# Moving the early decode of seven weight halves to later units of the attention loop

## The chip, the cores and the metric

The kernel runs on one core of a Trainium2 chip. The metric is the device time of one execution in microseconds (us), as the median of three runs. The profiled execution is a single one with its own time. Engines are named as in the profile: PE (matmul), PEld (weight load), DVE (VectorE), ACT (ScalarE), POOL (GpSimd), SP (the engine that issues most DMAs).

## The reference, cut to what matters

Three layers follow each other: attention with rotary embedding (2 batches, 8 heads, 576 positions, 64 per head), a dense layer with softplus, and a mixture of 8 experts.

```
q_rot, k_rot = rotate(q), rotate(k)
scores = q_rot @ k_rot.T / sqrt(64); attn = softmax(scores); x = attn @ v     # [2, 8, 576, 64]
h = x @ w_in                      # x: [1152, 512], w_in: [512, 2048]
g = max(h, 0) + log1p(exp(-abs(h)))
x = g @ w_out                     # w_out: [2048, 512]
# then per token: skip gate, best of 8 experts, relu(x @ w1[e]) @ w2[e], scaled, added to x
```

The inputs w_in and w_out come as 64-bit floats. The kernel loads them as pairs of 32-bit words and makes 32-bit floats of them by shifts and masks; this is the decode of the change. Each decoded value is then split into a high and a low part of PE's rounded 32-bit type, so that products keep their precision.

## The kernel before

The attention works on 8 pairs of heads, (b, hp) = (0,0) to (1,3), and in each pair on 5 units of up to 128 query rows, so on 40 units, numbered 0 to 39. A pair is 5 units: unit 10 is the first of pair (0,2), unit 25 the first of (1,1), unit 35 the first of (1,3). For each unit PE makes the scores of two heads (s, L253), DVE takes the row maximum of each (m, L262), ACT the exponential (P, L275), PE transposes P (t, L344), ACT and DVE copy the transposed pieces out (pt, L88 and L90), and PE multiplies by v (pv, L388). DVE scales the result (x, L397). There are two buffers for scores.

The order on PE, DVE, ACT and SP inside a unit is written out by hand:

```
ORDER = "S0 R T0 M0 K H0 E0 S1 T1 M1 L E1 H1 W J T2 N H2 Q".split()
```

S is scores, M the maximum, E the exponential, T transposes, H copies, J the products with v, Q the preparation of the next pairs. Step W calls `side(i)`, which runs the jobs that the table W_AT gives to unit i. The preparation includes DMAs on SP that restack the keys and queries of the next pair inside SBUF: ks (4 DMAs of 288 KB, L219) and qs (4 of 128 KB); the scores of the next pair read both. POOL does the rotary embedding (rt, rot, remr) and some small steps.

W_AT has seven entries ((f, x), units). f is a block of 128 of the 2048 hidden columns, x = 0 is its part of w_in, x = 1 that of w_out. The units are those of the jobs load, decode (z = 0), decode (z = 1), high, low; the last three entries have only load and decode. The jobs are:

```
nc.vector.tensor_scalar(tu, hi, 3, 0x3FFFFFFF, ...)             # L549, decode z = 0
nc.vector.scalar_tensor_tensor(tu, hi, 0xC0000000, tu, ...)     # L550, decode z = 0
nc.vector.scalar_tensor_tensor(tu, lo, 29, tu, ...)             # L552, decode z = 1
self.nc.scalar.copy(self.w[f][:, x, 0, :], self.t[f, x])        # L557, high
self.nc.vector.tensor_sub(w[:, 1, :], self.t[f, x], ...)        # L561, low
```

A load (L536, L538) is one DMA of 512 KB on SP into a tile raw. There are two raw buffers and three of the decoded tile wt. The load's place on SP's queue is not the unit of the table: a scheduler puts a DMA where its buffer is free, and SP then issues in that order, waiting where it must.

After the last unit the dense layer begins. Its first matmuls (L583) use the halves decoded in the attention. High and low of the last three entries, and all of the other 25 halves, follow there.

Of the kernel before, what the change touches and what calls it, by code (L numbers as in the profile page):

```python
# [30 lines left out]
MORE = (2, 0, 8, 8, 0)  # L31

W_AT = (
    ((0, 0), (6, 10, 11, 11, 12)), ((0, 1), (8, 13, 14, 14, 15)), ((1, 0), (12, 16, 17, 17, 18)),
    ((1, 1), (15, 19, 20, 20, 21)), ((2, 0), (18, 22, 23)), ((3, 0), (21, 25, 26)), ((2, 1), (24, 28, 29)),
)

WARM = (15, 4, 4, 3, 6, 3)
# [1223 lines left out]
```

## Time and profile before

| | us |
|---|---|
| median of 3 runs | 523.63 |
| lowest to highest | 523.41 to 524.08 |
| profiled execution, its own time | 525.89 |
| its span, first to last instruction | 524.1 |
| PE busy in the span | 494.2 |
| DVE busy | 394.1 |
| ACT busy | 349.4 |
| POOL busy | 124.7 |

The busy times are sums over stages with different limits. The span is what the trace shows; the execution's own time has 1.8 us more around it. Times inside the trace are us from the span's start.

### The profile page before, as it was taken

What the parts mean: (1) busy time and instruction counts of PE and PEld (TensorE: products, weight loads), DVE (VectorE), ACT (ScalarE), POOL (GpSimd) and SP (SyncE); (2) the same over time, 40 slices, a digit from 0 to 9 for tenths busy, and PEclk for the clock granted to TensorE, in tenths of its full rate; (3) what the DMA queues carried; (4) which work ended last, traced back from release to release, by engine and by line L of the source; (5) the groups of instructions that cost most, each with busy time, mean ns of one, the idle gap of its engine ahead of it and who ended that gap; (6) DMA issues with size and microseconds to landing.
All of it is one profiled execution on the core that took longest, in us unless ns stands there. A gap on an engine that the chain in (4) does not pass through costs nothing. (4 is left out here: it accounts for less than half of the span.)

```text
span 524.1 us, 8652 instructions
## 1 busy us (share of the span) xinstructions
PE 494.2 (94%) x2926; PEld 397.4 (76%) x2927; DVE 394.1 (75%) x703; ACT 349.4 (67%) x802; POOL 124.7 (24%) x165
## 2 busy tenths in 40 slices
PE   7998989989899989999999999999989899999994
PEld 3676766667677668999999998998966577777773
DVE  7675898988765697899888965548855678787873
ACT  2575676766676668787777877666944487676860
POOL 0965796667122200000000000010002301220112
PEclk9999899999999999999999999999997999999998
DMA  7269576487420230233333323203253605995201
GB/s 168 74 175 223 131 218 170 109 229 170 125 70 2 85 93 33 81 121 121 120 117 110 106 72 110 91 2 106 81 174 82 273 1 202 324 336 150 80 21 38
DMA packets 41604, 65.47 MB, mean 125 GB/s; under 512 B 9184, under 2 KB 23776, under 8 KB 41552
## 3 DMA queue, kind: packets, MB, share of 16 engines
q1 hardware_dynamic: 37776, 57.89, 37.7%
q0 software_dynamic: 1440, 4.20, 2.2%
q10 hardware_dynamic: 2336, 2.74, 1.7%
q8 instruction: 26, 0.43, 0.3%
q14 instruction: 26, 0.21, 0.1%
HBM read 67.30 MB, written 7.15 MB: 142 GB/s over the span
## 5 line engine op out<-in xcount | busy, mean ns | idle before, releaser
L583 PE MATMUL h<-xh,w 128*128 128x320 f32 (+2 forms) x464 | 105.1, 309 | 0.0
L621 PE MATMUL acc<-w,gh 128*128 128x512 f32 x288 | 79.1, 397 | 4.5 <-ACT gh L611 4.5
L842 DVE TENSOR_TENSOR ws<-raw,ws 128x1024 fp32r<-128x1024 f32 x59 | 70.3, 1221 | 16.7 <-ACT ws L840 16.6
L583 PEld LDWEIGHTS h<-xh,w 128*128 128x128 f32 x464 | 78.0, 188 | 3.5 <-ACT r L598 0.3
L583 PE MATMUL h<-xl,w 128*128 128x320 f32 (+2 forms) x232 | 69.4, 308 | 0.0
L621 PEld LDWEIGHTS acc<-w,gh 128*128 128x128 f32 x288 | 51.7, 188 | 15.7 <-ACT gh L611 7.0
L262 DVE TENSOR_REDUCE m<-s 128x1 f32<-128x576 f32 x64 | 47.8, 752 | 19.7 <-PE s L253 16.1
L840 ACT CAST ws<-raw 128x1024 fp32r<-128x1024 f32 x59 | 59.2, 1060 | 2.4 <-DMA raw<-in_moe_w_dram 1.9
L930 PE MATMUL y<-ws,hT 128*128 128x512 f32 x216 | 59.8, 415 | 0.9 <-DVE ws L842 0.2
L275 ACT ACTIVATE P<-s,m 128x576 f32<-128x576 f32 x64 | 47.6, 749 | 15.9 <-DVE m L262 15.7
L596 ACT ACTIVATE y<-h 128x320 f32<-128x320 f32 (+2 forms) x58 | 25.4, 440 | 38.9 <-PE h L583 36.8
L253 PE MATMUL s<-ks,qs 128*128 128x288 f32 x224 | 44.3, 320 | 6.3 <-issue 2.5
L930 PEld LDWEIGHTS y<-ws,hT 128*128 128x128 f32 x216 | 39.2, 188 | 13.3 <-DVE ws L842 2.3
L344 PE MATMUL t<-ct,P 128*128 128x128 f32 x288 | 45.8, 278 | 3.2 <-ACT pt L88 2.1
L684 POOL TENSOR_SCALAR sc<-lg 128x2 f32<-128x2 f32 (+1 forms) x3 | 0.9, 291 | 196.8 <-DVE lg L667 196.8
L583 PEld LDWEIGHTS h<-xl,w 128*128 128x128 f32 x232 | 43.2, 188 | 2.1
L621 PE MATMUL acc<-w,gl 128*128 128x512 f32 x144 | 44.2, 392 | 0.1
L612 DVE TENSOR_TENSOR gl<-r,gh 128x256 fp32r<-128x256 f32 (+2 forms) x42 | 25.8, 614 | 22.7 <-ACT gh L611 21.8
L344 PEld LDWEIGHTS t<-ct,P 128*128 128x128 f32 x288 | 34.0, 141 | 10.3 <-issue 3.0
L253 PEld LDWEIGHTS s<-ks,qs 128*128 128x128 f32 x224 | 32.0, 191 | 11.8 <-ACT P L275 4.9
L88 ACT COPY pt<-t 128x384 f32<-128x384 f32 x60 | 28.1, 481 | 17.5 <-PE t L344 17.4
L388 PE MATMUL pv<-pt,vr 128*64 128x256 f32 (+1 forms) x256 | 37.1, 412 | 0.0
(264 smaller groups left out, 956.0 us busy)
## 6 DMA issues: line engine op xcount, KB each, us to landing
raw<-in_moe_w_dram SPq DMA_DIRECT2D x68, 512.0 KB
raw<-in_moe_w_in_dram SPq DMA_DIRECT2D x16, 512.0 KB
raw<-in_moe_w_out_dram SPq DMA_DIRECT2D x16, 512.0 KB
ks<-kT SPq DMA_DIRECT2D x28, 288.0 KB
qs<-qT SPq DMA_DIRECT2D x28, 128.0 KB
wr<-in_moe_w_dram SPq DMA_DIRECT2D x5, 512.0 KB
x2d<-x SPq DMA_DIRECT2D x9, 256.0 KB
xn<-in_q_dram SPq DMA_DIRECT2D x8, 256.0 KB
```

Source lines behind the costliest of these rows:

```text
L88: self.nc.scalar.copy(out, in_)
L253: nc.tensor.matmul(ps[:, c, 0:288], lhsT=qs[:, a, uc], rhs=ks[:, a, x, 288 * c : 288 * c + 288], start=x == 0, stop=x == 1,)
L262: self.last = nc.vector.tensor_reduce(st["m"][:, a : a + 1], st["ps"][a][:, :, 0:288], axis=AX.XY, op=ALU.max, negate=True)
L275: nc.scalar.activation(P[:, 576 * a : 576 * a + 576].rearrange("p (c n) -> p c n", c=2), ps[:, :, 0:288], AF.Exp, bias=m[:, a : a + 1], ac ...
L344: self.tail = nc.tensor.transpose(ps[:, 128 * i : 128 * i + 128], src, ident)
L388: nc.tensor.matmul(ps[r, 0:n], lhsT=v, rhs=pt[:, k, 0:n], start=i < 0, stop=i == 3, skip_group_check=True,)
L583: nc.tensor.matmul(ps[c][:, 0:m], lhsT=w[:, 0, x, 128 * k : 128 * k + 128], rhs=src[:, k, c0 + m * c : c0 + m * c + m], start=z == 0, stop ...
L612: self.last = nc.vector.tensor_sub(gl, r, gh.bitcast(F32))
L621: nc.tensor.matmul(acc[t], lhsT=g[x][:, 128 * j : 128 * j + 128], rhs=w[:, 1, y, :], start=f == f0 and z == 0, stop=f == f1 and z == 2,)
L840: hi = nc.scalar.copy(w[:, 0], raw)
L842: self.did[T, c] = hi.ins, nc.vector.tensor_sub(w[:, 1], raw, w[:, 0].bitcast(F32)).ins
L930: nc.tensor.matmul(py, lhsT=ht[:, x, o : o + 128], rhs=w[:, y, 512 * j : 512 * j + 512], start=c == 0 and j == 0 and z == 0, stop=c == 3 a ...
```

## The change

The seven entries keep their jobs and their order; the units move later. A half that was loaded at unit 6 and decoded at 10 and 11 has its load at 18 and its decode at 24 and 25, and so on; the last decode moves from unit 29 to 37.

```
 W_AT = (
-    ((0, 0), (6, 10, 11, 11, 12)), ((0, 1), (8, 13, 14, 14, 15)), ((1, 0), (12, 16, 17, 17, 18)),
-    ((1, 1), (15, 19, 20, 20, 21)), ((2, 0), (18, 22, 23)), ((3, 0), (21, 25, 26)), ((2, 1), (24, 28, 29)),
+    ((0, 0), (18, 24, 25, 25, 26)), ((0, 1), (20, 26, 27, 27, 28)), ((1, 0), (25, 28, 29, 29, 30)),
+    ((1, 1), (27, 30, 31, 31, 32)), ((2, 0), (29, 32, 33)), ((3, 0), (31, 34, 35)), ((2, 1), (33, 36, 37)),
 )
```

The first place is SP's queue where the stacks for pair (0,2) are issued (ks_513 and its qs; xn is the natural q and k of a later pair). Before, two loads of weights stand among them:

```order
L219 DMA ks_513<-kT_512 64x2x576 x4
L536 DMA raw_556<-in_moe_w_in_dram 128x4x128
L219 DMA qs_576<-qT_575 64x512
L538 DMA raw_682<-in_moe_w_out_dram 128x512
L219 DMA qs_576<-qT_575 64x512 x3
L106 DMA xn_645<-in_q_dram 128x2x256
L106 DMA xn_645<-in_k_dram 128x2x256
```

Now the same place has none:

```order
L219 DMA ks_513<-kT_512 64x2x576 x4
L219 DMA qs_574<-qT_573 64x512 x4
L106 DMA xn_643<-in_q_dram 128x2x256
L106 DMA xn_643<-in_k_dram 128x2x256
L117 DMA vr_692<-in_v_dram 128x256
```

The two loads have left the place between ks and the last qs. Where they went is the second place, on SP's queue ahead of the stacks of pair (0,1) (ks_299); it is far ahead of unit 18, where the table has the first load. Now:

```order
L106 DMA xn_240<-in_q_dram 128x2x256
L106 DMA xn_240<-in_k_dram 128x2x256
L536 DMA raw_1229<-in_moe_w_in_dram 128x4x128
L538 DMA raw_1322<-in_moe_w_out_dram 128x512
L219 DMA ks_299<-kT_298 64x2x576 x4
L219 DMA qs_357<-qT_356 64x512 x4
```

Before, xn_240 was followed by ks_299 at once. The third place is DVE's queue in pair (1,2), around the maximum of its unit m (m12m). Before:

```order
L262 TENSOR_REDUCE m_1924<-s_1929 128x1
L212 TENSOR_TENSOR kT_1902<-tq_1897,kT_1902 128x512
L90 COPY pt_1914<-t_1934 128x3x128
L296 TENSOR_SCALAR sm_1878<-sm_1878 128x4
L297 RECIPROCAL sm_1878<-sm_1878 128x4
L262 TENSOR_REDUCE m12m<-s12m_1969 128x1
L262 TENSOR_REDUCE m_2036<-s_2021 128x1
L212 SCALAR_TENSOR_TENSOR qT_1963<-tq_1958,qT_1963 128x512
L90 COPY pt_1914<-t_1987 128x3x128
L397 TENSOR_TENSOR x_2013<-pv_1946,rb_2009 128x320
L262 TENSOR_REDUCE m_2036<-s_2042 128x1
```

Now, at the end of that stretch:

```order
L262 TENSOR_REDUCE m12m<-s12m_1954 128x1
L262 TENSOR_REDUCE m_2025<-s_2010 128x1
L212 SCALAR_TENSOR_TENSOR qT_1948<-tq_1943,qT_1948 128x512
L90 COPY pt_1895<-t_1972 128x3x128
L561 TENSOR_TENSOR w_1817<-wt_1870,w_1817 128x512
L549 TENSOR_SCALAR wt_1983<-raw_1819 128x512
L550 SCALAR_TENSOR_TENSOR wt_1983<-raw_1819,wt_1983 128x512
L397 TENSOR_TENSOR x_2002<-pv_1931,rb_1998 128x320
L262 TENSOR_REDUCE m_2025<-s_2031 128x1
```

Three decode instructions stand ahead of the scaling x and the maximum m, where none stood before.

Behind the attention the queues differ in one place of the part that runs: in the expert layer ACT's second ReLU (L902) and a cast of weights (L840, 1.06 us on average) swap places, and four transposes of tokens (L861) on PE stand four matmuls earlier. The branches for more than nine token tiles are ordered differently too; nine tiles run.

## Rows read from the trace of the kernel before

**Rows 1.** Busy us and instructions per engine, PE clock, DMA share, GB/s, pair by pair.

```profile
32.43:52.71 20.28, 17.25 (x133) 13.25 (x131) 12.74 (x26) 13.03 (x35) 11.60 (x16) 1.00 0.76 192
52.71:71.78 19.07, 18.90 (x132) 15.03 (x132) 16.88 (x28) 12.06 (x32) 15.50 (x17) 0.91 0.67 167
71.78:93.08 21.30, 18.48 (x138) 13.84 (x136) 19.31 (x35) 15.54 (x41) 15.63 (x21) 1.00 0.65 181
93.08:113.49 20.41, 18.00 (x136) 13.62 (x134) 17.91 (x34) 14.73 (x41) 13.14 (x16) 1.00 0.65 161
113.49:132.54 19.05, 17.62 (x132) 13.40 (x133) 16.05 (x29) 12.96 (x35) 12.25 (x16) 1.00 0.70 175
132.54:150.54 18.00, 17.36 (x132) 13.37 (x133) 11.39 (x23) 12.97 (x35) 3.51 (x7) 1.00 0.52 127
150.54:168.63 18.09, 17.80 (x136) 13.57 (x135) 11.48 (x25) 13.30 (x36) 4.16 (x10) 1.00 0.01 2
```

**Rows 2.** The same columns for PE (first), PEld, DVE, ACT, POOL in three stretches.

```profile
16.00:23.70 7.70, 7.18 (x45) 5.27 (x44) 5.34 (x11) 5.48 (x14) 7.70 (x10) 1.00 0.03 11
40.00:52.70 12.70, 10.21 (x81) 7.72 (x80) 7.10 (x13) 7.59 (x20) 7.07 (x8) 1.00 0.98 235
52.70:56.50 3.80, 3.79 (x19) 3.77 (x20) 1.94 (x4) 1.59 (x4) 1.07 (x3) 0.57 0.87 230
```

**Rows 3.** SP's timeline: start, us, instruction, count.

```profile
13.64 0.47 SPq L106 DMA_DIRECT2D xn<-in_k_dram  x1
23.71 3.79 SPq L219 DMA_DIRECT2D ks<-kT  x4
...
38.82 4.18 SPq L219 DMA_DIRECT2D ks<-kT  x4
43.04 0.84 SPq L536 DMA_DIRECT2D raw<-in_moe_w_in_dram  x1
...
45.52 0.58 SPq L538 DMA_DIRECT2D raw<-in_moe_w_out_dram  x1
46.20 1.76 SPq L219 DMA_DIRECT2D qs<-qT  x3
```

**Rows 4.** PE's timeline: start, us, instruction, [idle before, what ended it].

```profile
32.43 0.76 PE L253 MATMUL s<-ks,qs 128*128 128x288 f32 x4
...
52.71 0.89 PE L253 MATMUL s<-ks,qs 128*128 128x288 f32 x4 [2.50 <-issue]
...
56.49 0.67 PE L166 MATMUL tq<-ct,rot 128*128 128x128 f32 x4
...
93.08 0.79 PE L253 MATMUL s<-ks,qs 128*128 128x288 f32 x4
...
95.32 0.60 PE L166 MATMUL tq<-ct,rot 128*128 128x128 f32 x4
```

**Rows 5.** Tile wt alone, DVE and ACT: pair (1,1), and pairs (0,2) to (1,1) summed.

```profile
113.49:132.54 19.05, 5.48 (x6) 0.00 (x0) 1.00 0.70 175
sum 79.83, DVE 22.14 ACT 2.48; mean DVE 5.54 ACT 0.62
```

**Rows 6.** Tile wt, whole trace: count, ns shortest/median/longest, first and last start.

```profile
L549 DVE TENSOR_SCALAR wt<-raw x32: 417/422/1003, 57.2 to 294.4; 128x512 uint32<-128x512 uint32 x32
L550 DVE SCALAR_TENSOR_TENSOR wt<-raw,wt x32: 678/687/1662, 58.4 to 296.1; 128x512 uint32<-128x512 uint32 x32
L552 DVE SCALAR_TENSOR_TENSOR wt<-raw,wt x32: 675/687/1750, 61.0 to 298.0; 128x512 uint32<-128x512 uint32 x32
...
L561 DVE TENSOR_TENSOR w<-wt,w x32: 673/686/962, 65.2 to 301.1; 128x512 fp32r<-128x512 f32 x32
```

**Rows 7.** DVE's timeline, in pair (0,3) and after the attention.

```profile
85.05 1.75 DVE L552 SCALAR_TENSOR_TENSOR wt<-raw,wt 128x512 uint32<-128x512 uint32 x1
86.72 1.41 DVE L262 TENSOR_REDUCE m<-s 128x1 f32<-128x576 f32 x2
...
174.83 1.29 DVE L561 TENSOR_TENSOR w<-wt,w 128x512 fp32r<-128x512 f32 x2 [5.99 <-ACT w L557]
```

## The prediction

> **What bounds the kernel now.** I read the table of windows with one window per pair first, since the change touches the attention only, and then the timelines of PE, SP and DVE where a window shows loss. In [rows 1] the reader should take three differences from each row: span less PE busy is PE's idle time, span less DVE busy is DVE's spare time, and the clock column shows where PE ran slower. The two last pairs, which hold no decode, take 18.00 and 18.09 us with PE idle for 0.64 and 0.29: there PE is the bound. The earlier pairs take 19.05 to 21.30. Pairs (0,3), (1,0) and (1,1) have PE idle for 2.82, 2.41 and 1.43 while DVE is 91, 88 and 84% busy. Pairs (0,1) and (0,2) have a loss of another kind. PE sits 2.50 us before the first scores of pair (0,2) [rows 4]; no engine holds it ("issue"), and just then the DMA engines are 98% busy [rows 2], with two weight loads of 512 KB on SP's queue between ks and the last three qs that these scores read [rows 3]. Behind the wait PE's granted clock is 0.57 on average for 3.80 us [rows 2]: it runs mostly at the lower of its levels, 1.2 GHz. After the attention the queues keep their order but for one swap in the expert layer, of a cast of 1.06 us and its neighbours (told with the change); I cost it at 0, with 1.06 either way as its bounds.
>
> **The part at units 5 to 10: the wait for qs.** The two loads leave this place. Would qs then be there in time? For pair (0,1) no load stands between: ks is first issued at 23.71, the scores start at 32.43 without a marked wait, so ks and qs need at most 8.72 us [rows 3, 4]. Counted from 38.82 that is 47.54, and PE is ready for these scores at 52.71 - 2.50 = 50.21. The wait goes whole: 2.50 us, with 2.67 to spare. With it goes the slow clock. From these scores to the transposes tq took 56.49 - 52.71 = 3.78 us; the same stretch one and two pairs later is broken by other work or clean, and the clean one, in pair (1,0), took 95.32 - 93.08 = 2.24 [rows 4]. Gain 1.54. The Trainium skill (TensorE: Matmul & The Clock Gate, Part 1: The HAM clock gate) says that an idle PE falls to half clock and that activity releases it again; the drop here, after the 2.50 us of idling, agrees. Sum of this part: 4.04, bounds 2.5 (the clock falls for another reason) and 4.04.
>
> **Where the two loads go.** They are issued behind xn at 13.64 + 0.47, so about 14.1 to 15.5. From 16.00 to 23.70 the DMA engines are 3% busy [rows 2]. 1.05 MB at the 235 GB/s of the busy stretch needs 4.5 us, so they land near 20.5, 3.2 before ks is issued at 23.71. Cost 0; without this cover up to 4.5.
>
> **Pairs (0,2) to (1,0): the decode leaves DVE.** In its undisturbed form a half costs DVE 0.422 + 0.687 + 0.687 = 1.80, and 0.686 more with its low part [rows 6]. Seven halves and four lows are 7 x 1.80 + 4 x 0.686 = 15.3. In the trace they took 22.14 [rows 5], 1.44 times that, since POOL is busy for 12.3 to 15.6 us of each of these pairs [rows 1]. The delay can be seen in one place: L552 takes 1.75 us at 85.05 and two maxima follow only at 86.72 [rows 7]. Pairs (0,3) and (1,0) idle PE for 2.82 and 2.41, the pair without decode (1,2) for 0.64: the excess is 2.18 + 1.77 = 3.95. Some of it may belong to work that only these pairs have, such as the remainder's transposes and four more evictions. Bounds 0 (all of it is other work) and 3.95; I take 3.1, about four fifths, because the DVE share is the one column in which these pairs differ most from the clean ones. Pair (0,2) gains nothing more: 18.90 of its 19.07 are PE busy already.
>
> **Pairs (1,1) to (1,3): the decode arrives.** Two halves (3.59 undisturbed) were here already, in pair (1,1), where they took 5.48 [rows 5]. New here or in unit 24 are 15.3 - 3.6 = 11.7 us of DVE work. By the table, units 25 to 29 get 5.65, units 30 to 34 get 6.06, units 35 to 37 get 2.48, unit 24 gets 1.11 (z = 0 is L549 and L550, z = 1 L552, low L561). DVE's spare time in pair (1,2) is 18.00 - 11.39 = 6.61, in (1,3) 6.61, in (1,1) 3.00 with its old decode in. So it fits, with little left in (1,2), and it lies in front of maxima (third place of the change), so each instruction that comes at a bad moment delays scores two steps later. Price per us of undisturbed decode, from both kinds of row: in (1,1) (1.43 - 0.64)/3.59 = 0.22; in (0,3) and (1,0), which by the table hold 4.3 and 3.2 us, 3.95/7.5 = 0.53. I take 0.22, since (1,1) is the neighbour and POOL, which stretched the early decode, is busy for only 3.51 and 4.16 us in the last two pairs [rows 1]: 11.7 x 0.22 = 2.6 lost. Bounds 0 and 11.7. What the late pairs pay depends on POOL. The Trainium skill (SBUF — State Buffer, Who interferes with whom) has a rule for it: a DVE instruction with two SBUF inputs and a POOL instruction that reads SBUF shut each other out for a whole instruction. L550 and L552 are of that kind and go from 0.69 to 1.66 and 1.75 here, as it says. By it (1,2) pays the undisturbed 6.06; were the factor 1.44 a property of the attention instead, it would pay 8.7, more than the 6.61 spare, and lose 2.1 more.
>
> ACT's four casts (2.48 in all [rows 5]) move as well; ACT has 5 us spare in each late pair, cost inside the price above. SP: the late loads wait for a raw buffer, and ks and qs of the next pair stand behind some of them, but the decode that frees the buffer lies in a unit before the one that makes ks or qs. Cost 0; else up to a 512 KB transfer (2.2 us) for each of three. The last decode is at unit 37, near 160; two loads of the dense layer then need some 5 us, and DVE idles until 174.83 before it wants them [rows 7], so the end of the attention is covered.
>
> **Sum.** -4.04 - 3.1 + 2.6 = -4.5 us: the span goes from 524.1 to 519.6, the profiled execution from 525.89 to 521.4. The median of the runs shown is 523.63, 2.26 below the profiled one, and I subtract from it: **519.1 us**.
>
> **The rivals.**
> 1. *The late decode costs the early rate*, 0.53 per us: 6.2 instead of 2.6, so -0.9: 522.7. For it: it comes as one half per two units, denser than before. Against: POOL is idle there. Chance 0.10.
> 2. *DVE's queue becomes the bound (slower).* If the late instructions never fall into DVE's gaps, all 11.7 us delay PE: -7.1 + 11.7 = +4.6: 528.2. It decides once the decode of a pair passes its spare time, 6.06 against 6.61 in (1,2). Against: those gaps stand between the maxima already. Chance 0.06. The Trainium skill (TensorE: Matmul & The Clock Gate, Architectural detail) says that DVE takes its queue strictly in order, which is what would make this happen; the maxima behind L552 at 86.72 agree.
> 3. *The early idle time isn't the decode's* but that of POOL or ACT: -4.04 + 2.6 = -1.4: 522.2. For it: ACT is 15.54 busy in (0,3). Chance 0.08.
> 4. *The late decode hides wholly*: -4.04 - 3.95 = -8.0: 515.6. For it: 6.61 spare. Chance 0.13.
> 5. *The change doesn't do what it says:* its loads come first of all rather than three units ahead, and if they hold up ks at 23.71 the wait moves to pair (0,1): up to 4.5 back, near 523.6. It decides where less than 1.05 MB moves between 14 and 23.71. Chance 0.03.
>
> **How the numbers follow.** The forecast has 0.60, its own range 517.4 (3.95 early, 0.15 per us late) to 520.9 (2.2 and 0.30). The range to hold the time 8 in 10 takes in rivals 3 and 4 and leaves out 1, 2 and 5, 0.19 together: 515.5 to 522.3. About 0.2% (1.05 us) is what can be told from no change here. Faster: 0.60 + 0.13 + 0.08 and a third of rival 1, 0.84; same 0.09 (the rest of 1, and 5); slower 0.07.
>
> **What would show it.** Right: no idle before the first scores of pair (0,2), clock 1.00 there; pairs (0,3) and (1,0) near 19.5 and 19; (1,1) to (1,3) longer by 0.5 to 1.3 each; L550 and L552 near 0.69 in the last two; all after the attention shifted as a block. Wrong: a wait before the first scores of pair (0,1) (rival 5), PE idle for over 2 us in (1,2) (1 or 2), early pairs unchanged (3), or a wait for raw at the start of the dense layer.

## The result, and the profile after

| | before | after |
|---|---|---|
| median in the comparison | 524.04 (523.41 to 525.00, 6 runs) | 518.70 (517.15 to 519.15, 6 runs) |
| profiled execution | 525.89 | 518.53 |
| its span | 524.1 | 516.7 |
| PE busy | 494.2 | 491.6 |
| DVE busy | 394.1 | 388.1 |
| POOL busy | 124.7 | 120.9 |

The changed kernel takes 0.989 of the time, 95% interval [0.9874, 0.9907]: 5.3 us less by the medians, against 4.5 forecast. In a second comparison, with other runs of both kernels (below as e9), the ratio was 0.9867 [0.985, 0.9885]. The profiled executions differ by 7.36 us, more than the medians, because the profiled one of before was a long one; times below that are taken from traces add up to this larger figure. Of the 7.36 us, 6.57 lie in the attention (the marks below) and 0.67 ahead of its first mark.

The windows by pair after, with the columns of [rows 1]:

```profile
31.93:49.64 17.71, 17.16 (x131) 13.21 (x131) 12.31 (x23) 12.49 (x34) 11.58 (x16) 1.00 0.70 178
49.64:67.41 17.77, 17.33 (x134) 13.48 (x132) 13.02 (x24) 12.72 (x36) 14.15 (x18) 1.00 0.64 161
67.41:86.18 18.77, 17.73 (x138) 13.83 (x136) 13.55 (x27) 13.82 (x39) 12.42 (x17) 1.00 0.54 135
86.18:104.11 17.93, 17.51 (x136) 13.57 (x134) 12.33 (x27) 13.34 (x39) 11.92 (x17) 1.00 0.58 144
104.11:123.49 19.38, 17.83 (x135) 13.43 (x134) 17.23 (x33) 13.74 (x36) 13.47 (x16) 1.00 0.64 169
123.49:143.31 19.82, 17.74 (x136) 13.40 (x134) 18.26 (x37) 15.57 (x41) 4.28 (x7) 1.00 0.63 162
143.31:161.39 18.08, 17.80 (x134) 13.55 (x134) 13.24 (x27) 12.53 (x34) 4.17 (x10) 1.00 0.21 64
```

Against [rows 1] the first pair (0,1), whose window ends with the wait for qs, fell from 20.28 to 17.71, (0,3) from 21.30 to 18.77 and (1,0) from 20.41 to 17.93. A pair's window ends with the first scores of the next pair, so it holds any wait before them. The decode's arrival shows in DVE's column: 17.23 and 18.26 us in (1,1) and (1,2). Pair (1,2) is the dear one, 18.00 before and 19.82 now, and (1,3) pays nothing. The clock is 1.00 in every pair.

PE's timeline after, at the first scores of pair (0,2), and at those of pair (1,3):

```profile
48.63 1.08 PE L388 MATMUL pv<-pt,vr 128*64 128x256 f32 x8
49.64 0.80 PE L253 MATMUL s<-ks,qs 128*128 128x288 f32 x4
...
51.91 0.60 PE L166 MATMUL tq<-ct,rot 128*128 128x128 f32 x4
...
143.31 0.76 PE L253 MATMUL s<-ks,qs 128*128 128x288 f32 x4 [0.90 <-DMA raw<-in_moe_w_out_dram]
```

The scores at 49.64 follow the products pv without a gap; the 2.50 us of [rows 4] are gone. The transposes tq come 2.27 us behind them, as the 2.24 that the forecast took from a clean pair. But the first scores of pair (1,3), at 143.31, have a gap of 0.90 that pair (1,3) had not before. SP's timeline shows why; first the place of the early loads, then the stacks of pair (1,3):

```profile
13.44 0.47 SPq L536 DMA_DIRECT2D raw<-in_moe_w_in_dram  x1
13.95 0.50 SPq L538 DMA_DIRECT2D raw<-in_moe_w_out_dram  x1
23.04 3.79 SPq L219 DMA_DIRECT2D ks<-kT  x4
...
130.59 3.81 SPq L219 DMA_DIRECT2D ks<-kT  x4
134.50 1.29 SPq L536 DMA_DIRECT2D raw<-in_moe_w_in_dram  x1
135.89 3.29 SPq L219 DMA_DIRECT2D qs<-qT  x4
```

The two early loads are issued at 13.44 and 13.95, nine us ahead of the first ks, and hold up nothing, as forecast. The load at 134.50, the raw of (3,0), stands between the ks and the qs of pair (1,3). It is the order of [rows 3], which cost 2.50 us there with two loads, now with one load and at unit 31 of 40. DVE's timeline shows the same landing from the other side:

```profile
142.03 0.43 DVE L549 TENSOR_SCALAR wt<-raw 128x512 uint32<-128x512 uint32 x1 [0.40 <-DMA raw<-in_moe_w_in_dram]
```

DVE stands at the decode of unit 34, with a maximum behind it, until that raw is there at 142.03. Which of the two waits costs the time is what two of the experiments below decide.

The kernel before had the same order at two more places, which the prediction does not name. By its SP timeline the load of (3,0) was issued between the ks and the qs of pair (1,1), and the first load of the halves that the dense layer decodes itself between those of pair (1,2):

```profile
104.27 1.34 SPq L536 DMA_DIRECT2D raw<-in_moe_w_in_dram  x1
105.71 3.28 SPq L219 DMA_DIRECT2D qs<-qT  x4
...
124.12 1.32 SPq L536 DMA_DIRECT2D raw<-in_moe_w_in_dram  x1
125.53 3.27 SPq L219 DMA_DIRECT2D qs<-qT  x4
```

PE's timeline of the kernel before, at the first scores of the two pairs:

```profile
113.49 0.77 PE L253 MATMUL s<-ks,qs 128*128 128x288 f32 x4 [0.85 <-DMA xn<-in_q_dram]
...
132.54 0.76 PE L253 MATMUL s<-ks,qs 128*128 128x288 f32 x4 [0.80 <-DMA vr<-in_v_dram]
```

In the changed kernel no load stands at these two places, and the scores at 104.11 and 123.49 follow without a gap. Counted from the last scores of the pair ahead, the way to the first scores is 3.66 and 3.61 us before and 2.57 in both places after: 1.09 and 1.04 less. No experiment moves these two loads alone. But over all the traces below, the eleven without a load at the place of pair (1,1) and the twelve without one at that of (1,2) show no such wait. The load does not always suffice: e1 below has one at the place of (1,1), and its scores are only 0.18 us late.

**Marks.** To compare kernels I take the start of the scores of unit m in each pair (tile s00m to s13m, L235) and the first matmul of the dense layer (h) from PE's timeline, and the time between one and the next. A mark of batch 0 lies 2 to 3 us before the next pair begins, one of batch 1 some 7 us after its own pair began; the stretch s11m to s12m therefore holds the last three fifths of pair (1,1) and the first two fifths of (1,2); the expectations call it (1,1), and the next one (1,2). The decode lies in the second to sixth stretch before, and in the fifth to eighth after.

| | s00m-s01m | -s02m | -s03m | -s10m | -s11m | -s12m | -s13m | -h | sum | ratio to before |
|---|---|---|---|---|---|---|---|---|---|---|
| before | 17.94 | 21.63 | 21.30 | 10.57 | 19.86 | 19.05 | 17.36 | 11.35 | 139.06 | |
| after | 18.10 | 17.77 | 18.78 | 9.94 | 18.21 | 19.51 | 18.82 | 11.36 | 132.49 | 0.9890 |
| e9 after, again | 18.18 | 17.76 | 18.82 | 9.94 | 18.21 | 19.51 | 18.95 | 11.37 | 132.74 | 0.9867 |
| e1 loads first | 18.24 | 17.96 | 21.93 | 9.99 | 18.96 | 19.04 | 17.38 | 11.35 | 134.85 | 0.9917 |
| e2 decode late | 18.05 | 21.25 | 18.78 | 9.95 | 18.21 | 19.51 | 18.93 | 11.35 | 136.03 | 0.9933 |
| e3 double | 18.21 | 17.78 | 18.79 | 9.94 | 18.18 | 22.25 | 18.55 | 11.37 | 135.07 | 0.9925 |
| e5 spread | 18.19 | 17.78 | 18.78 | 9.95 | 19.30 | 18.78 | 18.21 | 11.36 | 132.35 | 0.9851 |
| e6 triple in (1,1) | 18.21 | 17.76 | 18.78 | 9.97 | 18.17 | 25.17 | 18.69 | 11.37 | 138.12 | 0.9955 |
| e7 triple in (1,2) | 18.14 | 17.78 | 18.78 | 9.94 | 18.22 | 19.51 | 20.71 | 11.37 | 134.45 | 0.9913 |
| e8 latest | 18.25 | 17.79 | 18.76 | 9.95 | 18.02 | 19.38 | 17.36 | 11.35 | 130.86 | 0.9844 |
| e10 from unit 30 | 18.22 | 17.78 | 18.77 | 9.95 | 18.01 | 18.01 | 18.51 | 11.34 | 130.59 | 0.9904 |
| e11 raw in time | 18.11 | 17.81 | 18.78 | 9.95 | 18.22 | 19.50 | 19.11 | 11.34 | 132.82 | 0.9857 |
| e12 load behind qs | 18.15 | 17.78 | 18.77 | 9.95 | 18.21 | 19.51 | 17.70 | 11.34 | 131.41 | 0.9860 |
| e13 best table | 18.10 | 17.81 | 18.77 | 9.95 | 18.02 | 18.50 | 17.69 | 11.35 | 130.19 | 0.9823 |

Stretches that a table doesn't change repeat within 0.15 us (0.3 in the first), so a difference of 0.2 in one of them can be read, which no median could show. Each row is one trace. Outside the marks s00m lies between 28.6 and 29.8 in all of them. From h to the end there are 355.5 us before and 355.3 after, but 353.7 in the second trace of the changed kernel (e9): one kernel differs by 1.7 us there between two executions, and the medians hold that too.

### The profile page after: what moved, and what is told of

Its sections match the earlier page's. It is cut to its first block, busy times and chain, and to the rows that moved or that the text cites. A ratio compares the mean times of both kernels' runs of the same rounds, so it can differ in the third digit from the quotient of the medians.

```text
span 516.7 us, 8662 instructions
## 1 busy us (share of the span) xinstructions
PE 491.6 (95%) x2926; PEld 395.9 (77%) x2927; DVE 388.1 (75%) x703; ACT 349.0 (68%) x802; POOL 120.9 (23%) x165
## 3 DMA queue, kind: packets, MB, share of 16 engines
q10 hardware_dynamic: 2336, 2.74, 1.7%
## 5 line engine op out<-in xcount | busy, mean ns | idle before, releaser
L840 ACT CAST ws<-raw 128x1024 fp32r<-128x1024 f32 x59 | 59.2, 1060 | 2.0 <-DMA raw<-in_moe_w_dram 1.9
```

The lines of the kernel that those rows point to most:

```text
L840: hi = nc.scalar.copy(w[:, 0], raw)
```

## The experiments

**The two parts apart.** e1 moves only the two first loads to the front and leaves every decode where it was; e2 leaves these two loads where they were and moves every decode.

```
e1  ((0, 0), (1, 10, 11, 11, 12)), ((0, 1), (1, 13, 14, 14, 15)),   the rest as before
e2  ((0, 0), (6, 24, 25, 25, 26)), ((0, 1), (8, 26, 27, 27, 28)),   the rest as after
```

> The first two loads go to the quiet stretch near 14 us and all decode stays at its old units. If the change has two separate parts, this gives the first alone: no idle before the first scores of pair (0,2) and no slow clock behind it, 4.0 us less than before, near 520.0, with pairs (0,3) and (1,0) still at some 21 and 20 us. If the loads alone do everything, it reaches the changed kernel, 518.7. If the decode alone does everything, it stays at 524.0.

> The two loads stand between ks and qs as before, and all decode moves to its new units. If the parts are separate: the 2.5 us wait and the slow clock stay, pairs (0,3) and (1,0) lose 5 us together as in the changed kernel, the late pairs gain 2, so 3.0 us less than before, near 521. If the loads alone do everything: the late price alone, 2 us slower, near 526.

e1 took 520.30 us, ratio 0.9917 [0.9902, 0.9933]; e2 520.59, 0.9933 [0.9912, 0.9954]. In e1 the second stretch falls from 21.63 to 17.96 and the early pairs stay long: s02m to s03m takes 21.93, where the changed kernel takes 18.78. The windows show DVE nearly full there, 20.63 of 21.93 us, and POOL busy for 17.55:

```profile
65.40:87.33 21.93, 18.49 (x139) 13.82 (x138) 20.63 (x35) 14.81 (x39) 17.55 (x22) 1.00 0.67 175
```

In e2 the wait stands where it stood, by PE's timeline:

```profile
52.44 0.77 PE L253 MATMUL s<-ks,qs 128*128 128x288 f32 x4 [2.59 <-issue]
```

The slow clock is behind it, in the windows by engine (PEclk is the third column from the end):

```profile
52.44:55.00 2.56, 2.56 (x17) 2.56 (x18) 1.75 (x4) 1.53 (x4) 1.07 (x3) 0.79 0.97 259
55.00:58.00 3.00, 3.00 (x18) 2.97 (x17) 1.53 (x3) 1.85 (x7) 0.84 (x1) 0.61 0.31 68
```

The clock of 0.79 and then 0.61 follows the wait and not the decode, which is far off in this kernel. From s00m to h, e1 gains 4.21 us and e2 3.03 against before; the two together 7.24, the changed kernel 6.57. The parts are nearly independent. The 0.67 between the sums lie mostly in s10m to s11m, which ends behind the first scores of pair (1,1): both e1 (18.96) and e2 (18.21) are rid of the wait that made it 19.86, so the two sums count it twice. e1 still has the load of (3,0) between ks and qs there and all of the decode; its way from the last scores of (1,0) to the first of (1,1) is 2.75 us in place of 3.66, which is the 0.90. From s02m to s10m, where the early decode lies as well, e1 takes 31.92 and the kernel before 31.87, the same.

**What a late decode instruction costs.** e3 issues the second shift-and-or (L552) of all seven halves twice.

```
-nc.vector.scalar_tensor_tensor(tu, lo, 29, tu, ...)
+for _ in range(2 if (f, x) in [e[0] for e in W_AT] else 1):
+    nc.vector.scalar_tensor_tensor(tu, lo, 29, tu, ...)
```

> The changed kernel with the last decode instruction of the seven early halves issued twice (the second changes no bit): 7 x 0.687 = 4.8 us more of DVE work in units 25 to 37. At the price of the prediction, 0.22 per us, 1.1 us slower than the changed kernel, near 519.8. If DVE's queue passes each instruction on to PE whole: 4.8 slower, 523.5. If the late pairs hide it: 518.7.

It took 520.58 us, 0.9925 [0.9906, 0.9943]. All of the price falls in one stretch, s11m to s12m: 22.25 in place of 19.51. (L552 is L553 in the rows of e3, e6 and e7, whose edit adds a line.) The next is even 0.27 shorter, though the doubled halves lie there as well. DVE's timeline, from the dear place:

```profile
117.10 2.89 DVE L553 SCALAR_TENSOR_TENSOR wt<-raw,wt 128x512 uint32<-128x512 uint32 x2
119.91 0.74 DVE L262 TENSOR_REDUCE m<-s 128x1 f32<-128x576 f32 x1
```

Two copies take 2.89 us where two undisturbed ones take 1.37 (twice the 0.687 of [rows 6]), and the maximum stands behind them. POOL is in the rotary embedding there (L129, of 1.72 and 1.26 us, at 117.71 and 120.22). So I put the same work in two places that differ in POOL: e6 triples L552 of the halves at units 25, 27 and 29, e7 of those at 31, 33 and 35.

```
e6  range(3 if (f, x) in ((0, 0), (0, 1), (1, 0)) else 1)
e7  range(3 if (f, x) in ((1, 1), (2, 0), (3, 0)) else 1)
```

> The changed kernel, with the second shift-and-or (L552, 0.69 us undisturbed) of the halves (0,0), (0,1) and (1,0) issued three times instead of once; no bit changes. These stand at units 25, 27 and 29, all in pair (1,1), where POOL is busy with the rotary embedding: 6 x 0.69 = 4.1 us more DVE work. Theory A, the price of a DVE instruction is set by POOL beside it: the rate of the doubled run was 2.74 us lost for 4.8 us put in, all of it in pair (1,1), so about 0.57 per us or more: this run loses 2.3 to 4 us against the changed kernel, about 521 to 522.5, and the copies last 1.2 to 1.7 us each. Theory B, the price is set by how full DVE is in the pair: spare DVE time of the changed kernel is 2.15 us here, so 4.1 - 2.15 = 2 us are lost at least, 520.5, with the copies near 0.69. The two differ in the other run of this pair of runs.

> The changed kernel, with L552 of the halves (1,1), (2,0) and (3,0) issued three times instead of once; no bit changes. These stand at units 31 and 33 in pair (1,2) and unit 35 in pair (1,3), where POOL is busy for 4.3 and 4.0 us only: again 4.1 us more DVE work, 2.7 of it in pair (1,2). Theory A (POOL beside it): the copies last 0.69 us and hide in DVE's gaps; lost 0 to 0.6 us, about 518.5 to 519. Theory B (how full DVE is): pair (1,2) has the least spare DVE time of all, 1.56 us, so 2.7 - 1.56 = 1.2 us are lost there at least, and by the forecast's 0.22 per us 0.9: 519.5 to 520.5.

e6 took 522.29 us, 0.9955 [0.994, 0.9971]; e7 519.35, 0.9913 [0.9893, 0.9932]; the changed kernel beside them 517.43. By the marks the same 4.1 us cost 5.66 in e6 (25.17 - 19.51) and 1.89 in e7 (20.71 - 18.82). Of e6's six extra copies two, at unit 25, lie ahead of s11m and cost nothing (18.17 in s10m to s11m, against 18.21). That the other four, 2.7 us, cost 5.66 has two steps. DVE's timeline of e6:

```profile
117.86 2.88 DVE L553 SCALAR_TENSOR_TENSOR wt<-raw,wt 128x512 uint32<-128x512 uint32 x2
120.67 0.74 DVE L262 TENSOR_REDUCE m<-s 128x1 f32<-128x576 f32 x1
121.34 1.45 DVE L553 SCALAR_TENSOR_TENSOR wt<-raw,wt 128x512 uint32<-128x512 uint32 x1
122.71 0.45 DVE L90 COPY pt<-t11m 64x64 f32<-64x64 f32 x2
```

POOL's timeline of e6 beside it, with a product and the sums of the rotary embedding (L126, L129):

```profile
117.25 1.27 POOL L126 TENSOR_TENSOR rot<-xn,cr 128x512 f32<-128x512 f32 x1
118.48 1.71 POOL L129 TENSOR_TENSOR rot<-rot,rt 128x512 f32<-128x512 f32 x1
...
120.98 1.26 POOL L129 TENSOR_TENSOR rot<-rot,rt 128x512 f32<-128x512 f32 x1
```

PE's timeline of e6, behind the copies:

```profile
123.30 0.87 PE L344 MATMUL t<-ct,P 128*128 128x128 f32 x3 [2.32 <-DVE pt L90]
```

And the windows of e6 by engine, behind that wait and over the whole stretch:

```profile
123.30:127.00 3.70, 3.70 (x16) 2.83 (x18) 3.70 (x7) 3.15 (x10) 1.33 (x2) 0.50 0.76 213
127.00:130.00 3.00, 3.00 (x20) 1.75 (x17) 2.48 (x6) 0.46 (x1) 0.00 (x0) 0.70 0.02 5
...
112.28:137.45 25.17, 21.71 (x139) 15.62 (x138) 23.26 (x41) 15.53 (x40) 10.60 (x12) 0.86 0.55 143
```

The same stretch in the changed kernel:

```profile
111.70:131.21 19.51, 17.70 (x135) 13.41 (x134) 18.03 (x35) 14.15 (x37) 10.35 (x12) 1.00 0.60 158
```

First, the copies take about 1.44 each, and the copy pt (L90) of the transposed probabilities stands behind the third at 122.71: PE is idle for 2.32 us until it has that piece. Second, behind this wait PE's granted clock is 0.50 for 3.70 us and 0.70 for 3.00: PE's busy time in the stretch is 21.71, against 17.70 in the changed kernel, 4.0 of the 5.66. In the first of the two windows that is 1.2 GHz throughout. The waits of 0.90 and 1.18 before pair (1,3) in other runs here had no such tail.

Theory A is right on the length of the copies in e6 and too low on their price, 2.3 to 4, for the slow clock was not in it. On e7 it is too hopeful, 0.6 at most; theory B's 1.2 or more holds there. In e7 the instructions were short (median of L552 0.684). All six extra copies start in s12m to s13m, and 4.1 us cost 1.89. Even that reading is kind: the 18.82 beside it holds the wait for qs of pair (1,3), and e7 has no wait before those scores. Against e12 below, which hasn't that wait either, they cost 3.01 (20.71 - 17.70). DVE's timeline of e7, where it stops:

```profile
136.49 0.69 DVE L212 SCALAR_TENSOR_TENSOR qT<-tq,qT 128x512 fp32r<-128x512 f32 x1 [1.90 <-ACT qT L153]
```

The windows of e7 by engine, for the stretch s12m to s13m:

```profile
131.48:152.19 20.71, 17.42 (x132) 13.08 (x130) 18.23 (x37) 13.20 (x35) 3.78 (x7) 1.00 0.52 134
```

DVE has 18.23 us of work there, more than the 17.36 that the stretch takes without decode, so some 0.87 are lost whatever the order. Besides, DVE stands 1.90 us at the low part of qT, which waits for ACT: ACT's queue has another order in e7, with qT at 135.84 behind an exponential and a cast, where the changed kernel has it at 132.73. So theory B has its part once DVE's work outgrows PE's, and with POOL idle too. Short of that the place decides, as the next runs show.

**Where the decode could lie.** Three tables, with the first two loads at the front. e5 gives each half three units from 20 on, e8 three units from 26 on with the last at 42 and 43, e10 two units from 30 on.

```
e5  ((0,0),(1,20,21,21,22)), ((0,1),(1,23,24,24,25)), ((1,0),(21,27,28,28,29)), ((1,1),(24,30,31,31,32)),
    ((2,0),(28,34,35)), ((3,0),(31,37,38)), ((2,1),(35,40,41))
e8  ((0,0),(1,26,27,27,28)), ((0,1),(1,29,30,30,31)), ((1,0),(27,32,33,33,34)), ((1,1),(30,35,36,36,37)),
    ((2,0),(33,38,39)), ((3,0),(36,40,41)), ((2,1),(39,42,43))
e10 ((0,0),(1,30,31,31,32)), ((0,1),(1,32,33,33,34)), ((1,0),(31,35,36,36,37)), ((1,1),(33,37,38,38,39)),
    ((2,0),(36,39,40)), ((3,0),(38,41,42)), ((2,1),(40,42,43))
```

> The loads first, and the decode spread thinner: one half in three units from unit 20 to 38, the last at 40 and 41, behind the last maximum. If the loss in pair (1,2) of the changed kernel (19.82 us against 18.00) comes from one half per two units, pair (1,2) falls to some 18.7 and the kernel to 517.5. If POOL's work in pairs (0,3) to (1,1) stretches the decode as much as before, what (1,2) gains is given back in (1,0): 518.7 or more.

> Only the table differs from the changed kernel: the first two loads stay at the front, and the decode goes further back, one half in three units from unit 26 on; the last decode is at units 42 and 43, behind the last maximum. Three halves (1,0), (1,1), (2,0) then lie in the pairs with an idle POOL, one less in pair (1,1), one and a half behind the attention's last maxima, where DVE has 6 us idle before the dense layer. Theory A (POOL beside it sets the price): pair (1,1) gets shorter by about 1 us against the run spread over three units, (1,2) and (1,3) no longer: 515.5 to 516.5. Theory B (how full DVE is): the last two pairs, and the start of the dense layer, now take what pair (1,1) gives: 517 to 518. If the dense layer's own loads then come late, because the two raw buffers are freed later, a wait for raw or w stands before its first or second block: up to 2.2 us for each, 519 or more.

> The changed kernel itself once more, on the same chip and with the same runs of the kernel before as the other three, so that these are compared with it there: ratio 0.989, near 518.5.

> Only the table differs: loads of (0,0) and (0,1) stay at the front, and all seven halves are decoded from unit 30 on, in 14 units to the last one, 43. Pair (1,1), units 25 to 29, then holds no decode at all, and pair (1,2) two halves and two low parts, about 5.0 us of DVE, as much as in the changed kernel, but with raws that landed early. Theory A (POOL beside it sets the price, and the changed kernel's loss in pair (1,2) is a late raw): (1,2) takes 17.4 us from the first scores of its unit m to those of the next pair, as with three units per half, (1,1) falls from 19.4 to 18 or less, the whole is 515 to 516. Theory B (how full DVE is): (1,2) takes 18.5 or more. Theory C (what pair (1,1) has lost was never the decode's): (1,1) stays at 19 to 19.4 without a decode, and the whole is within 0.5 us of the run spread over three units from unit 26, about 516.5. If the dense layer waits for the last halves: 518 or more.

e5 took 517.13 us, 0.9851 [0.9833, 0.987]; e8 516.46, 0.9844 [0.9822, 0.9867]; the changed kernel beside e8 517.43, 0.9867 [0.985, 0.9885]; e10 519.10, 0.9904 [0.9882, 0.9927]. In e5 the stretch s10m to s11m is 1.09 us longer (19.30 against 18.21). Most of it is no price of the decode: this table has the load of (1,0) at unit 21, and SP issued it at 97.12, between the ks (93.21) and the qs (98.51) of pair (1,1). PE's timeline of e5 has a wait there that the trace puts down to qs:

```profile
105.67 0.76 PE L253 MATMUL s<-ks,qs 128*128 128x288 f32 x4 [0.73 <-DMA qs<-qT]
```

From the last scores of (1,0) to these it is 3.54 us in place of 2.57, 0.97 of the 1.09. Two stretches answer the question, s11m to s12m and s12m to s13m. The windows of e8:

```profile
111.39:130.77 19.38, 17.84 (x135) 13.43 (x134) 15.19 (x30) 14.40 (x37) 9.70 (x12) 1.00 0.61 159
130.77:148.13 17.36, 17.07 (x131) 13.00 (x130) 15.31 (x32) 13.79 (x36) 3.91 (x7) 1.00 0.52 129
```

The second row is the clean case. DVE does 15.31 us there, 4.2 more than the 11.13 of the kernel before, which had no decode in that stretch, and PE's time is the same to the hundredth: 17.36. With POOL at 3.91 and DVE's work 2.05 short of the stretch, the decode hides wholly. The first row has the same decode (4.52 us of tile wt, against 4.53) and the same DVE (15.19), but POOL at 9.70. What it costs there, e10 shows. Theory A had expected that stretch about 1 us shorter than in e5; it is 0.60 longer (19.38 against 18.78). e10 puts only three decode instructions into the first stretch, late in it, as its windows show:

```profile
112.49:130.50 18.01, 17.38 (x135) 13.38 (x134) 12.77 (x24) 13.45 (x35) 8.78 (x12) 1.00 0.47 112
130.50:149.01 18.51, 17.36 (x132) 13.05 (x130) 16.01 (x33) 14.42 (x37) 3.71 (x7) 1.00 0.60 150
```

18.01 against 19.38. So theory C falls: what the stretch has lost is the decode's, 1.37 us for the 2.86 us of it that e8 has more there (4.52 against 1.66 in the windows of tile wt). Of theory A's numbers for e10 the first held (18.0) and the second not: s12m to s13m takes 18.51, not 17.4, with 0.58 us of idle time before the first scores of pair (1,3); e10 has a load between ks and qs there, as the changed kernel has, and e8 hasn't. And e10's 130.59 from s00m to h, the shortest till then, were given back behind h, as the last case of its expectation has it (518 or more), by PE's timeline of e10:

```profile
179.21 3.06 PE L621 MATMUL acc<-w,gh 128*128 128x512 f32 x8 [3.52 <-ACT gh L611]
```

The dense layer's second step waits 3.52 us for gh, behind a DVE that is still decoding: at 166.00 it had stood 1.94 us for a raw whose load was issued at 162.56 only, when the L552 of 161.65 had freed its buffer. e8 idles 1.68 at that place, the changed kernel 1.23.

**Which wait is the loss of pair (1,2).** e11 delays the decode that stood waiting for raw by one unit and moves no load; e12 does so too and puts the load of (3,0) behind the qs.

```
after  ((3, 0), (31, 34, 35)), ((2, 1), (33, 36, 37))
e11    ((3, 0), (31, 35, 36)), ((2, 1), (33, 37, 38))
e12    ((3, 0), (32, 35, 36)), ((2, 1), (34, 37, 38))
```

> The changed kernel with the last two decodes one unit later: (3,0) at units 35 and 36 in place of 34 and 35, (2,1) at 37 and 38 in place of 36 and 37. No load moves on SP's queue. The raw of (3,0) landed at 142.0 and the decode of unit 34 stood waiting for it at the head of DVE's queue, with the maximum behind it. Theory A (this wait is the loss of pair (1,2)): (1,2) gets shorter by about 0.9 of its 1.46 us, from 18.8 to 18.9 to about 17.9, and (1,3) stays at 11.36 from its unit m to the dense layer: the whole is 0.9 us faster, 0.9850 of the kernel before where the changed kernel had 0.9867. Theory B (how full DVE is): half a half moves from (1,2) to (1,3), 1.1 us at 0.22, so 0.25 us: (1,2) at 18.5 or more.

> The kernel with the last two decodes one unit later, and besides the load of (3,0) at unit 32 in place of 31 and that of (2,1) at 34 in place of 33: on SP's queue the load of (3,0) then stands behind the four qs of pair (1,3) in place of between ks and qs. DVE's order is the same as in the run before. Theory D (the loss of pair (1,2) in the changed kernel is the old wait for qs come back: PE waits for the qs that stand behind a 512 KB load): the wait of 0.90 to 1.18 before the first scores of pair (1,3) goes, and (1,2) takes 17.4 to 17.9 us between the marks of unit m in place of 18.8 to 19.1; the whole is 1.2 us faster than the changed kernel, 516.0 to 516.3 where that has 517.4. Theory B (how full DVE is): another wait takes its place and (1,2) stays at 18.5 or more. If the raw of (3,0) then comes too late for unit 35, DVE waits in pair (1,3) and that pair gets longer than 11.36 from its unit m on.

e11 took 517.20 us, 0.9857 [0.9831, 0.9884]; e12 516.75, 0.9860 [0.9837, 0.9882]. The medians don't part them; the traces do. In e11 DVE no longer waits for raw, and PE's gap is there all the same, even longer, by PE's timeline:

```profile
144.23 0.76 PE L253 MATMUL s<-ks,qs 128*128 128x288 f32 x4 [1.18 <-DMA raw<-in_moe_w_out_dram]
```

s12m to s13m took 19.11. Theory A missed it, and theory B, whose bound of 18.5 or more holds it, had it 0.25 shorter and not 0.29 longer. What stays the same from the changed kernel to e11 is SP's order. e12 changes that, by SP's timeline:

```profile
130.73 3.78 SPq L219 DMA_DIRECT2D ks<-kT  x4
134.61 3.95 SPq L219 DMA_DIRECT2D qs<-qT  x4
138.60 0.59 SPq L536 DMA_DIRECT2D raw<-in_moe_w_in_dram  x1
```

The windows of e12 by engine, for the stretch s12m to s13m:

```profile
131.36:149.06 17.70, 17.12 (x131) 13.03 (x130) 15.71 (x32) 13.41 (x35) 3.71 (x7) 1.00 0.60 156
```

The stacks are issued in one piece, the gap is gone, and the stretch takes 17.70: 1.12 less than in the changed kernel (1.25 less than in e9) and 1.41 less than in e11, from which it differs by the place of loads alone. The trace's own word for the gap, "DMA raw", misled me here: the scores read ks and qs. At the like waits of other runs the trace names qs (e5), xn and vr (before). The Trainium skill (DMA: Bandwidth & Descriptors, Queues, rings and completion order) says that each DMA engine takes the descriptors of a ring in ring order, and that SP's queue has one ring on each. By that, 512 KB ahead of qs delay qs, and e12 agrees.

**A better table.** e13 puts together what the runs had shown: the first two loads at the front, decode from unit 28 on, where POOL has done with the rotary embedding, no load between ks and qs, the last half at unit 42.

```
e13 ((0,0),(1,28,29,29,30)), ((0,1),(1,30,31,31,32)), ((1,0),(29,33,34,34,35)), ((1,1),(32,35,36,36,37)),
    ((2,0),(34,37,38)), ((3,0),(36,39,40)), ((2,1),(38,41,42))
```

> Only the table differs from the changed kernel: the first two loads at the front; the decode from unit 28 on, where POOL has done with the rotary embedding, one half in two units, the last at 41 and 42; no load between ks and qs. What the runs so far say each part is worth: pair (1,1) at 18.0 when it holds no decode, 19.4 with the halves of units 26 to 29; pair (1,2) at 17.36 with two halves and no late qs; the dense layer begins without the wait of 3.5 us that the table from unit 30 on had at its start, since the last half is decoded one unit earlier. If these add up: (1,1) 18.0 to 18.5, (1,2) 17.4, 515 to 515.8 for the whole. If the decode in units 28 and 29 costs what it did in 25 to 27 (price not set by POOL): (1,1) 19 or more, 516.5. If the dense layer waits as in the table from unit 30 on: 518 or more.

It took 515.27 us (514.88 to 515.32), 0.9823 [0.9805, 0.984], the fastest of all: 9.4 us below the median of before beside it (524.70). Its windows:

```profile
111.67:130.17 18.50, 17.56 (x135) 13.36 (x134) 15.73 (x28) 13.77 (x36) 9.42 (x12) 1.00 0.56 138
130.17:147.86 17.69, 17.15 (x131) 13.01 (x130) 15.72 (x31) 13.73 (x35) 4.11 (x7) 1.00 0.62 157
```

The first stretch holds 5.23 us of decode and takes 18.50. The kernel before took 19.05 there with 3.06 us, but 1.04 of that is its wait before pair (1,2); its decode, at units 28 and 29, cost next to nothing. The 0.49 left of e13 against the 18.01 of e10 go most likely to the first two instructions, at 118.5 and 119.3, which take 0.77 and 1.25 us beside POOL's split of x into xh and xl. The second stretch took 17.69 where 17.4 was expected. Against the ratios of the changed kernel, 0.9890 and 0.9867, the table of e13 saves another 0.4 to 0.7%.

## Why the prediction came out right, and where it didn't

The forecast was 519.1 us, range 515.5 to 522.3; the median was 518.70. By the marks, the attention gained 6.57 us where the sum said 4.5. Its mechanisms were at work, but two waits that it did not see are mixed into two of its terms. The terms, one by one:

- **Wait for qs and slow clock: -4.04 forecast.** Measured 3.86 in the stretch s01m to s02m (21.63 to 17.77); e1, where the loads alone move, has 3.67 of it. e1 and e2 show that both parts go with the loads and come back with them. Right.
- **The early loads at 0.** Right: issued at 13.44, no wait before the first scores of pair (0,1); rival 5 is out.
- **The early decode: -3.1, bounds 0 to 3.95.** Measured 4.80 in its stretches: 2.52, 0.63 and 1.65 in s02m to s11m (21.30 to 18.78, 10.57 to 9.94, 19.86 to 18.21). Of the last, 1.09 are the wait for qs before pair (1,1), so the decode's own share is 3.7; from e1 to the changed kernel it is 3.95 (50.88 to 46.93). The mechanism was right: e2, which moves the decode, has the whole gain (51.73 to 46.94), and e1, which doesn't, only 0.85 of it, by that wait. But the 3.95 of the bound, PE's idle time in (0,3) and (1,0), held 0.85 of waiting for qs. That the decode's share came out inside it all the same is luck in part: from [rows 1] to the rows after, the idle time of the two pairs fell by 3.77 and PE's busy time by another 1.24, which the forecast had counted as work. Rival 3 is out.
- **The late decode: +2.6, bounds 0 to 11.7.** Measured 1.92 (0.46 in s11m to s12m, 1.46 in s12m to s13m, 0.01 behind): near in size, and wrong in what it is. The 0.46 are 1.50 for the decode less the 1.04 of the old wait before (1,2); the 1.46 are 1.12 for the new wait before (1,3) (e12) and 0.34 for the decode. The decode's own price is thus 1.84, or 0.16 per us of the 11.7. The 0.22 of the forecast had another source: PE's idle time of (1,1) in [rows 1] is 0.79 above that of (1,2), and the wait at 132.54, at the end of that window, is 0.80. A wait for qs was read as the decode's price. That the decode, put into (1,1), then costs 0.25 per us (1.50 more in the changed kernel than in e10, which has 5.95 us less of it there) is a coincidence. In e8 pair (1,2) pays nothing for 4.53.
- **SP's late loads at 0, else up to 2.2 us for each of three.** This is the step that failed, and in both directions. I argued from the units that a load behind which ks and qs stand would be issued in time; one of the three was, by the order of the program, between ks and qs, and its place on the queue was enough to cost 1.12. The order of SP's queue could be seen ahead of the run, and the waits of the kernel before in its trace. I read the queue at the place from which the loads went and not at the places to which they went, nor at the two other places in the kernel before where a load stood between ks and qs. With those the change of SP's order gained 1.09 + 1.04 - 1.12, about 1.0 us, where the forecast had 0.
- **Rival 2, DVE's queue as the bound,** is what e3 and e6 make by hand: instructions ahead of a maximum or a copy, 2.74 and 5.66 us lost. The changed kernel stays short of it in the pair that I had named, (1,2), and is nearest to it in (1,1), where the same instructions take longer. The sign that the prediction gave for rivals 1 and 2, PE idle for over 2 us in (1,2), did appear: 19.82 - 17.74 = 2.08. But 0.90 of it is the wait for qs, of which neither rival speaks, and e12, which differs from e11 by loads alone, takes 1.41 less there.
- **Rivals 1 and 4.** The late decode pays 0.16 per us against the 0.53 of rival 1, which is out; rival 4, a late decode that hides wholly, is right for (1,3), nearly right for (1,2) once no qs is late (0 in e8, 0.34 in e12), and wrong for (1,1).

The errors of the terms mostly point one way: 0.6 too little gain from the early decode, 0.8 too much loss from the late one and 1.0 from waits that were not in the sum, less 0.3 at the first wait and ahead of it, make about the 2.1 between 4.5 and 6.57. That the median came so near to the forecast is owed in part to the runs: this comparison gave 5.3 and the second one 6.8 (524.26 to 517.43). The forecast of (1,1) to (1,3) longer by 0.5 to 1.3 each was off in the same way as the late term: by windows (1,1) has 0.33 more, (1,2) 1.82 and (1,3) nothing.

That POOL makes the dear places dear rests most on e8, where the same decode beside the same DVE work costs 1.37 (against e10) with POOL at 9.70 and nothing with POOL at 3.91, and on e3 and e6, whose copies took 1.44 us each beside POOL's instructions. The Trainium skill (SBUF — State Buffer, Who interferes with whom) gives a mechanism: a DVE instruction with two SBUF inputs and a POOL instruction that reads SBUF exclude each other. The 1.44 for 0.69 in e6 agrees. No run here took POOL's work away from beside an unmoved decode, so that step is argued, not shown. And POOL's busy time in a stretch is not the whole of it: the kernel before had POOL at 8.85 in s11m to s12m and paid next to nothing for its 3.06 us of decode there, e6 paid nothing for its two extra copies in s10m to s11m with POOL at 12.77 of 18.17 us, and e7 paid 3.01 for 4.1 with POOL at 3.78. What stands behind the instruction on DVE's queue, and how full DVE is, have their part.

## What to carry to other kernels

Filler work on an engine is priced by the place and not by the amount: put it where the engine beside which it was seen to take longer is idle, where its own engine has time to spare, and where nothing urgent stands behind it on its queue. 4.5 us of it cost nothing in one stretch of e8, and 2.7 us cost 5.7 in one of e6, 4.0 of them by PE's slower clock. A load that is moved has two places to check on its queue, the one it leaves and the one it comes to; look for a small urgent transfer behind it. Before the idle time of a window is charged to the work in it, look in the timeline where that time lies: the 0.79 us that priced the late decode here was a wait at the window's end. And compare stretches between fixed marks of the trace rather than medians: e11 and e12 have the same median within 0.5 us, and 1.4 us between them in one stretch.

## What was not expected

A wait of PE can cost more than itself: the 2.32 us in e6 were followed by 6.7 us at granted clocks of 0.50 and 0.70, while 0.90 and 1.18 us before pair (1,3) were followed by 1.00. And the table's unit of a load doesn't set its place: the loads of units 18 and 20 were issued at 13.4 and 14.0, ahead of all stacks. A free buffer doesn't explain that alone, for the same two loads, at units 6 and 8 of the table, stayed at 43.04 and 45.52 in the kernel before with the same buffers free; no run shows what does. The load at unit 31, one unit earlier than e12's, cost a pair 1.12 us.
